# A cached attention step with an MLP gate: the prologue's q product through four PSUM banks, another order of the weight loads and of the gate product, another order at the exit

## The chip, the core and the metric

The kernel runs on one core of one Trainium2 chip. The metric is device time in microseconds (us) of one execution, lower is better. The engines are TensorE (PE in the profile; its weight loads are PEld), VectorE (DVE), ScalarE (ACT), GpSimd (POOL) and SyncE (SP), which here does little but issue DMA transfers. Each engine works through its own instructions in order, and semaphores hold them against each other.

## What is computed

Two sequences of one token each (B = 2, D = 512) go through an attention step over a long cache and, beside it, through a small MLP whose result gates the attention's output:

```
xn = layernorm(x)
q  = xn @ wq                                  # 512 x 4096: 32 heads of 128
p  = softmax(q k^T / sqrt(128));  o = p v     # 8 kv heads, 4 q heads on each, 32768 keys
s  = o @ wo                                   # 4096 x 512
m  = xn + gelu(layernorm(xn) @ w3) @ w4       # the MLP
out = x + s * silu(m)
```

The MLP has a first half with `w1` and `w2`, whose result is shifted along the sequence; with one token that leaves only zeros, so the kernel does not load these weights. k_cache and v_cache are 2 x 8 x 32768 x 128 in bf16, 134 MB each; wq and wo have 4.2 MB each, w3 and w4 1.8 MB each.

## The kernel before, in words

**Groups.** The 16 pairs of a sequence and a kv head are the groups. For each group the kernel loads K (8.4 MB) and V (8.4 MB). K goes into two of the three slots of `kbuf` (a group takes two neighbouring slots, alternately 0 and 1, or 1 and 2); V takes both slots of `vbuf`. In each group, VectorE transposes K in 16 pieces (L632) into four small buffers `T`, TensorE multiplies them with q into two PSUM banks `sc` (L744), VectorE takes maxima (L611) and a row from which the softmax shift follows (L754, L643), ScalarE takes the exponential (L534), VectorE transposes that (L651), TensorE multiplies it with V into the PSUM bank `o` (L766) and sums the weights into the bank `S` (L773), and ScalarE copies `o` out (L539). The head's division and turning (`head_on`, `head_xp`, `head_out`) come one group later.

**The order of the transfers.** SP issues all large transfers on one queue, in the order written down: w3 (L327), w4 (L328), wq (L329), K of group 0 (L330), V of group 0 (L495), four small ones that spread the gate g (L504), and then K and V by turns (L511, L495), at the end wo in six parts (L524, L526). wq lies in slot 2 of `kbuf`, w3 and w4 in `vbuf`. Each issue waits for the buffer that it overwrites:

- V of group 0 waits for the w4 product (`e_h2`, L501), since it overwrites w3 and w4.
- K of group m waits until the first half of group m-1 is through TensorE (L513); K of group 1 waits for `e_q` too, since wq lies under it.
- V of group m waits for ScalarE's signal at L538 that group m-1's product with V is done.

Below, K0, V0, K1, V1 and so on are these transfers, by their group.

**The prologue** (L327 to L506) makes everything that group 0 needs. VectorE clears PSUM banks (L351 to L356), makes two layernorms (L358 to L376) and a number of constant masks. TensorE turns the normalized rows (L416) and makes the w3 product into the bank `pro` (L425). VectorE transposes that out of PSUM (L429) and goes through the gelu (L430 to L437, the tanh on ScalarE at L435). TensorE makes the w4 product into a bank of `sc` (L449 to L451), VectorE and ScalarE make the gate g from it (L452 to L454). Only then the q product: a loop of eight chunks of 512 columns (L463), four matmuls each, through the two `sc` banks by turns; ScalarE copies each chunk into the buffer `q_row` (L477, L479), which GpSimd had cleared (L345); after the last copy VectorE transposes it in four instructions of 32 x 1024 (L481). L483, L487 and L490 bring q into its final form `qr`, from which GpSimd fills the weights `z` of group 0 (L549). `order(m)` says which half of K comes first.

**The exit** (L783 to L817). After the last group TensorE takes the head's last turn (`head_xp`, L785), a product of all earlier heads' outputs named wide (L787), a filler (L790), and then the products with wo (L805, L813), each part as it lands; `own_part` (L672) turns wide into the left operand of the first part on VectorE. wsum (L691) and L795 join the two accumulations; L692, L693 apply the gate and add x; two transfers write the output (L696).

`Queue.op` (L50) adds the waits that an instruction needs and signals a count of its engine; `LateQueue` (L67) keeps TensorE's prologue instructions until `place()` (L730). `take(s, n)` (L411) waits until semaphore s has n and lowers it by n.

Of the kernel before, what the change touches and what calls it, by code (L numbers as in the profile page):

```python
# [21 lines left out]
T_BUFS = 4  # L22
# [109 lines left out]
def kernel(  # L132
# [48 lines left out]
    def sb(name, shape, dt):  # L181
        return pool.tile(shape, dt, name=name)
# [7 lines left out]
    T_all = sb("T", [128, T_BUFS * W], I32)  # L190
    Ts = [T_all[:, i * W:(i + 1) * W] for i in range(T_BUFS)]
# [51 lines left out]
    sc2 = bank("sc", 512 * NPART)  # L243
    sc = [sc2[:, 512 * i:512 * (i + 1)] for i in range(NPART)]
    o = bank("o")
    S = bank("S")
# [56 lines left out]
    qT = kbuf_wq.bitcast(F32)[:, 0:Hq * 32]  # L303
    q_row = T_all[0:32, :].bitcast(F32)
    assert T_BUFS * W == Hq * Dh
# [18 lines left out]
    with tc.tile_critical(sync_engine=mybir.EngineType.Pool, no_gpsimd_drain=True):  # L324
        nc.scalar.wait_ge(t_shift, n_out).then_inc(t_shift, -n_out)

        sp.op(lambda e: e.dma_start(out=vbuf[:, 0:W4O], in_=B_w3.rearrange("(p k) f -> p (k f)", k=DK)), inc=(d_w3, 16))  # L327
        sp.op(lambda e: e.dma_start(out=vbuf[:, W4O:W4O + FK * D], in_=B_w4.rearrange("(p f) d -> p (f d)", f=FK)), inc=(d_w4, 16))  # L328
        sp.op(lambda e: e.dma_start(out=kbuf_wq[:, 0:DK * HD], in_=A_wq.rearrange("(p k) f -> p (k f)", k=DK)), inc=(d_wq, 16))  # L329
# [15 lines left out]
        e_row0 = po.op(lambda e: e.memset(q_row, 0.0))  # L345
# [5 lines left out]
        ve.op(lambda e: e.memset(o[:, :], 0.0))  # L351
        for t in (S[:, 0:NPART * rep], oT[:, :]):
            ve.op(lambda e, t=t: e.memset(t, 1.0), inc=(t_tv, 1))
        e_pro0 = ve.op(lambda e: e.memset(pro[:, :], 0.0))
        ve.op(lambda e: e.memset(sc[0][:, :], 0.0))
        e_s00 = ve.op(lambda e: e.memset(sc[1][:, :], 0.0))  # L356
        nc.vector.sem_inc(t_q, NPART)
# [71 lines left out]
        e = ve.op(lambda v: v.transpose(out=h4[:, :], in_=pro[:, 0:FQ]), e, e_row0)  # L429
# [7 lines left out]
        e = ve.op(lambda v: v.tensor_mul(out=h_bf[:, :], in0=hf[:, :], in1=th[:, :]), e, (d_w4, 16))  # L437
        h2 = sc[1]
# [10 lines left out]
        pe.op(lambda t: t.matmul(h2[0:B, :], lhsT=h_bf[:, 0:B], rhs=w4v[:, 0, :], start=True, stop=False), e, inc=False)  # L449
        pe.loop(nc, (FK - 2) // W4N, w4_part)  # L450
        e_h2 = pe.op(lambda t: t.matmul(h2[0:B, :], lhsT=h_bf[:, (FK - 1) * B:FK * B], rhs=w4v[:, FK - 1, :], start=False, stop=True))  # L451
        e_tf = ve.op(lambda v: v.tensor_add(out=t_f[:, :], in0=xn[:, :], in1=h2[0:B, :]), e_h2)  # L452
        e = ac.op(lambda v: v.activation(out=sig[:, :], in_=t_f[:, :], func=ACT.Sigmoid), e_tf)
        e_g = ve.op(lambda v: v.tensor_mul(out=g[:, :], in0=t_f[:, :], in1=sig[:, :]), e)  # L454

        HC = 512 // Dh
        NC = Hq // HC

        def q_part(t, c):
            take(t, t_q)  # L460
            out_c = sc2[0:B, bass.ds((c & 1) * 512, 512)]
            for k in range(DK):
                ins = t.matmul(  # L463
                    out_c, lhsT=xT[:, k, :], rhs=wq3[:, k, bass.ds(c * 512, 512)],
                    start=(k == 0), stop=(k == DK - 1))
            return ins

        pe.loop(nc, NC, q_part, e_tf, (d_wq, 16), inc=(t_qp, 1))

        def q_out(c):  # L470
            take(nc.scalar, t_qp)
            return q_row[0:B, bass.ds(c * 512, 512)], sc2[0:B, bass.ds((c & 1) * 512, 512)]

        ac.wait(e_row0)
        with nc.Fori(0, NC - 1, engines=[ACTE]) as c:
            dst, src = q_out(c)
            nc.scalar.copy(out=dst, in_=src).then_inc(t_q, 1)  # L477
        dst, src = q_out(NC - 1)
        e = ac.op(lambda v: v.copy(out=dst, in_=src))  # L479
        for n in range(NQ):  # L480
            e = ve.op(lambda v, n=n: v.transpose(  # L481
                out=qT[32 * n:32 * n + 32, :], in_=q_row.rearrange("p (h n y) -> p n h y", n=NQ, y=32)[:, n, :, :]), e, e_row0)
# [372 lines left out]
```

## Time and profile before

| | |
|---|---|
| time, median of 3 runs | 657.93 us (657.11 to 658.06) |
| the profiled execution's own time | 658.21 us |
| its span from the first to the last instruction | 656.4 us |
| busy share of the span: PE, PEld, DVE, ACT, POOL | 65%, 24%, 59%, 7%, 2% |
| DMA: bytes, rate over the span, share of 16 engines on SP's queue | 280.53 MB, 427 GB/s, 98.9% |
| granted TensorE clock, mean | 0.885 |

The span starts with the first instruction; all times of rows are counted from there. A row of the timeline gives the start, the duration, the engine, the line, the operation, the written and the read tile, the shapes, the number of instructions merged into the row, and in brackets how long the engine had been idle and what ended that. A row of the stage table gives the stretch and its length, the busy time of each engine with its number of instructions, and at its end the granted TensorE clock, the DMA engines' share and the rate in GB/s. "DMA share" and GB/s of a short stretch swing because a packet counts where it begins.

### The profile page before, as it was taken

To read this page: it belongs to the slowest core of one execution; us is meant where nothing else is said; L and a number is where in the kernel's file an instruction comes from. 1 tells how busy PE (TensorE), PEld (TensorE's weight loads), DVE (VectorE), ACT (ScalarE), POOL (GpSimd) and SP (SyncE) were. 2 spreads that over 40 slices of the span, in tenths; PEclk is the share of its full clock that TensorE was granted. 3 is DMA by queue.
4 is the path that set the end of the run, shared out by engine and by line. 5 is a ranking of instruction groups with operands and counts; after the bars stand their busy time and mean duration, and the time that the engine had idled before them with its cause. 6 is when DMAs were issued, how large, how long until landed. Compare 5 with 4: busy or idle time off the path is not lost. (4 is left out here: it accounts for less than half of the span.)

```text
span 656.4 us, 6559 instructions
## 1 busy us (share of the span) xinstructions
PE 427.7 (65%) x2411; PEld 160.5 (24%) x2443; DVE 386.9 (59%) x543; ACT 44.3 (7%) x98; POOL 14.0 (2%) x45
## 2 busy tenths in 40 slices
PE   1628687474866757487675748757575875658876
PEld 0103232122322222132222213222222322223323
DVE  6169393573928557292754828376382846738772
ACT  1220101000010000101000010100001010000101
POOL 3000000000000000000000000000000000000000
PEclk9879979698897979889796988969699796969999
DMA  9999999999999999999999999999999999999996
GB/s 374 425 447 448 403 423 443 439 427 423 439 439 443 423 423 443 439 439 427 423 443 435 439 431 419 447 435 435 435 419 443 439 431 435 423 443 415 437 427 263
DMA packets 6246, 280.53 MB, mean 427 GB/s; under 512 B 730, under 2 KB 868, under 8 KB 1380
## 3 DMA queue, kind: packets, MB, share of 16 engines
q1 hardware_dynamic: 6232, 280.50, 98.9%
q8 instruction: 1, 0.02, 0.0%
q14 instruction: 1, 0.01, 0.0%
q10 hardware_dynamic: 12, 0.00, 0.0%
HBM read 280.50 MB, written 0.00 MB: 427 GB/s over the span
## 5 line engine op out<-in xcount | busy, mean ns | idle before, releaser
L632 DVE STREAM_TRANSPOSE T<-kbuf 128x1024 int32<-128x1024 int32 x256 | 296.5, 1214 | 165.0 <-DMA kbuf<-in_A_k_cache_dram 148.4
L744 PE MATMUL sc<-T,z 128*128 128x512 bf16 x992 | 271.9, 421 | 160.9 <-PEq L412 156.6
L744 PEld LDWEIGHTS sc<-T,z 128*128 128x128 bf16 x1024 | 98.5, 103 | 327.6 <-issue 238.5
L766 PE MATMUL o<-vbuf,pt 128*16 128x512 bf16 x1024 | 70.8, 379 | 17.7 <-PEq L412 17.7
L534 ACT ACTIVATE ep<-sc,shift 128x512 bf16<-128x512 f32 x32 | 21.7, 682 | 495.4 <-ACTq L412 495.4
L766 PEld LDWEIGHTS o<-vbuf,pt 128*16 128x16 bf16 x1024 | 27.5, 88 | 64.6 <-issue 42.4
L611 DVE TENSOR_REDUCE mx<-sc 128x1 f32<-128x512 f32 x32 | 21.5, 672 | 34.4 <-PE xp L711 34.4
L718 PE MATMUL pro<-ob,comb 128*2 128x512 f32 x66 | 33.7, 592 | 0.0
L651 DVE STREAM_TRANSPOSE pt<-ep 128x512 bf16<-128x512 bf16 x32 | 22.6, 707 | 15.0 <-ACT ep L534 15.0
L754 PE MATMUL S<-mxr,same_h 128*128 128x448 f32 x32 | 15.8, 576 | 18.3 <-PEq L412 18.3
L705 PEld LDWEIGHTS oT<-sel_o,ob 128*128 128x128 f32 x128 | 15.5, 191 | 11.1 <-issue 11.1
L705 PE MATMUL oT<-sel_o,ob 128*128 128x4 f32 x128 | 16.4, 252 | 0.0
L773 PE MATMUL S<-sm,ones_f 128*128 128x448 f32 x32 | 16.3, 592 | 0.0
L539 ACT COPY ob<-o 128x512 f32<-128x512 f32 x16 | 9.4, 585 | 78.6 <-ACTq L412 78.6
L556 POOL COPY oX<-oXs 128x4 bf16 (+1 forms) x16 | 3.0, 186 | 545.1 <-POOLq L412 545.1
L643 DVE TENSOR_REDUCE shift<-S 128x1 f32<-128x64 f32 x16 | 3.6, 224 | 14.3 <-PE S L754 14.3
L481 DVE STREAM_TRANSPOSE kbuf<-T 32x1024 f32<-32x1024 f32 x4 | 4.9, 1235 | 10.7 <-ACT T L479 10.6
L463 PE MATMUL sc<-kbuf,xT 128*2 x32 | 8.2, 377 | 3.8 <-issue 2.3
L754 PEld LDWEIGHTS S<-mxr,same_h 128*128 128x128 f32 x32 | 4.8, 188 | 22.6 <-issue 22.6
L615 DVE TENSOR_SCALAR mxr<-row_of,mx 128x32 f32<-128x32 f32 x32 | 7.7, 242 | 1.1
L416 PE MATMUL qrb<-ident,xs_bf 34*128 34x34 bf16 x4 | 0.3, 198 | 12.0 <-DVE xs_bf L376 12.0
L718 PEld LDWEIGHTS pro<-ob,comb 128*2 128x2 f32 x66 | 4.2, 83 | 14.0 <-issue 10.4
(106 smaller groups left out, 96.3 us busy)
## 6 DMA issues: line engine op xcount, KB each, us to landing
kbuf<-in_A_k_cache_dram SPq DMA_DIRECT2D x2, 4096.0 KB, 21.9
vbuf<-in_A_v_cache_dram SPq DMA_DIRECT2D x2, 4096.0 KB, 21.2
kbuf<-in_A_wq_dram SPq DMA_DIRECT2D x1, 4096.0 KB, 20.6
vbuf<-in_B_w_dram SPq DMA_DIRECT2D x2, 1792.0 KB, 9.5
kbuf<-in_A_wo_dram SPq DMA_DIRECT2D x1, 2048.0 KB, 30.2
kbuf<-in_A_wo_dram SPq DMA_DIRECT2D x3, 512.0 KB, 31.4
kbuf<-in_A_wo_dram SPq DMA_DIRECT2D x1, 384.0 KB
kbuf<-in_A_k_cache_dram SPq DMA_DIRECT2D x15, 26.7
```

What stands on the lines that cost most here:

```text
L463: ins = t.matmul(out_c, lhsT=xT[:, k, :], rhs=wq3[:, k, bass.ds(c * 512, 512)], start=(k == 0), stop=(k == DK - 1))
L534: nc.scalar.activation(out=ep[i][:, :], in_=sc[i][:, :], func=ACT.Exp, scale=inv_sqrt_dh, bias=shift[:, :], accum_out=rs[:, i:i + 1]).then ...
L539: nc.scalar.copy(out=ob[:, :], in_=o[:, :]).then_inc(t_ob, 1)
L611: ins = nc.vector.tensor_reduce(out=mx[:, i:i + 1], in_=sc[i][:, :], axis=AX.X, op=ALU.max)
L632: ins = nc.vector.transpose(out=Ts[n % T_BUFS][:, :].rearrange("p (b t k) -> p t b k", b=NB, t=RT), in_=kt[:, r * W:(r + 1) * W].rearrange ...
L651: ins = nc.vector.transpose(out=pt[h][:, :, :].rearrange("p r (t h) -> p t r h", h=rep), in_=ep[order(par).index(h)][:, :].rearrange("p (t ...
L705: ins = nc.tensor.matmul(oT[:, :], lhsT=ob[:, t * Dh:(t + 1) * Dh], rhs=sel_o[:, t, :], start=(t == 0), stop=(t == VT - 1))
L718: nc.tensor.matmul(pro[0:B, :], lhsT=comb[:, 0:B], rhs=ob[:, :], start=True, stop=True)
L744: ins = nc.tensor.matmul(sc2[:, bass.ds(i * 512, 512)], lhsT=z[:, nb, w, zc:zc + 128], rhs=Tb[:, nb, :, w], start=(r == 0 and nb == 0 and ...
L754: nc.tensor.matmul(S[:, NPART * rep:NPART * (rep + SREP * 32)].rearrange("p (s c) -> p s c", s=SREP), lhsT=same_h[:, :], rhs=mxr[:, :, :]. ...
L766: ins = nc.tensor.matmul(o[32 * j:32 * j + VT * rep, :], lhsT=pt[h][:, r, a * VT * rep:(a + 1) * VT * rep], rhs=vt[:, u * VT:(u + 1) * VT, ...
L773: nc.tensor.matmul(S[:, 0:SSUM * NPART * rep].rearrange("p (s c) -> p s c", s=SSUM), lhsT=ones_f[:, :], rhs=sm[:, :, :].rearrange("p i h - ...
```

## The change

Four things are changed.

1. **q goes through four PSUM banks, and VectorE takes it from there.** The banks `sc` (2), `o` and `S` become one tile `banks`, and chunk c of the q product goes into bank c mod 4, with room for four at the start. When two chunks are done, VectorE transposes them straight out of PSUM, in four instructions of 32 x 256, into `qT`, which now lies in the first of the `T` buffers; ScalarE's eight copies, `q_row` and GpSimd's clearing of it are gone. The clearing of `S` and `o` moves behind the gate.
2. **The loads are issued in the order w3, wq, w4.**
3. **The gate product (w4) comes behind the q product on TensorE**, into the bank `pro`. On VectorE the gate's operations come behind those of q, up to `qr`.
4. **At the exit the wide product and the filler come ahead of the last head's turn**, and TensorE's extra wait at the end of each group (L779) is gone.

```diff
-    T_all = sb("T", [128, T_BUFS * W], I32)
-    Ts = [T_all[:, i * W:(i + 1) * W] for i in range(T_BUFS)]
+    Ts = [sb(f"T{i}", [128, W], I32) for i in range(T_BUFS)]
...
-    sc2 = bank("sc", 512 * NPART)
+    QB = 4
+    banks = bank("banks", 512 * QB)
+    sc2 = banks[:, 0:512 * NPART]
     sc = [sc2[:, 512 * i:512 * (i + 1)] for i in range(NPART)]
-    o = bank("o")
-    S = bank("S")
+    o, S = (banks[:, 512 * i:512 * (i + 1)] for i in (2, 3))
...
-    qT = kbuf_wq.bitcast(F32)[:, 0:Hq * 32]
-    q_row = T_all[0:32, :].bitcast(F32)
-    assert T_BUFS * W == Hq * Dh
+    qT = Ts[0].bitcast(F32)
...
         sp.op(lambda e: e.dma_start(out=vbuf[:, 0:W4O], in_=B_w3.rearrange("(p k) f -> p (k f)", k=DK)), inc=(d_w3, 16))
+        sp.op(lambda e: e.dma_start(out=kbuf_wq[:, 0:DK * HD], in_=A_wq.rearrange("(p k) f -> p (k f)", k=DK)), inc=(d_wq, 16))
         sp.op(lambda e: e.dma_start(out=vbuf[:, W4O:W4O + FK * D], in_=B_w4.rearrange("(p f) d -> p (f d)", f=FK)), inc=(d_w4, 16))
-        sp.op(lambda e: e.dma_start(out=kbuf_wq[:, 0:DK * HD], in_=A_wq.rearrange("(p k) f -> p (k f)", k=DK)), inc=(d_wq, 16))
...
-        e_row0 = po.op(lambda e: e.memset(q_row, 0.0))
...
-        ve.op(lambda e: e.memset(o[:, :], 0.0))
-        for t in (S[:, 0:NPART * rep], oT[:, :]):
-            ve.op(lambda e, t=t: e.memset(t, 1.0), inc=(t_tv, 1))
         e_pro0 = ve.op(lambda e: e.memset(pro[:, :], 0.0))
-        ve.op(lambda e: e.memset(sc[0][:, :], 0.0))
-        e_s00 = ve.op(lambda e: e.memset(sc[1][:, :], 0.0))
-        nc.vector.sem_inc(t_q, NPART)
+        ve.op(lambda e: e.memset(oT[:, :], 1.0), inc=(t_tv, 1))
+        e_s00 = ve.op(lambda e: e.memset(banks[0:32, :], 0.0), inc=(t_q, QB))
...
-        e = ve.op(lambda v: v.transpose(out=h4[:, :], in_=pro[:, 0:FQ]), e, e_row0)
+        e = ve.op(lambda v: v.transpose(out=h4[:, :], in_=pro[:, 0:FQ]), e)
...
-        e = ve.op(lambda v: v.tensor_mul(out=h_bf[:, :], in0=hf[:, :], in1=th[:, :]), e, (d_w4, 16))
-        h2 = sc[1]
+        e_hb = ve.op(lambda v: v.tensor_mul(out=h_bf[:, :], in0=hf[:, :], in1=th[:, :]), e)
+        HC = 512 // Dh
+        NC = Hq // HC
+        QP2 = 2 * HC
+
+        def q_part(t, c):
+            take(t, t_q)
+            out_c = banks[0:B, bass.ds((c & (QB - 1)) * 512, 512)]
+            for k in range(DK):
+                ins = t.matmul(
+                    out_c, lhsT=xT[:, k, :], rhs=wq3[:, k, bass.ds(c * 512, 512)],
+                    start=(k == 0), stop=(k == DK - 1))
+            return ins
+
+        q_0 = pe.n
+        pe.loop(nc, NC, q_part, e_xT, (d_wq, 16))
+        for c in range(NC // 2):
+            two = banks[0:32, 1024 * (c % 2):1024 * (c % 2) + 1024].rearrange("p (h n y) -> p n h y", n=NQ, y=32)
+            for n in range(NQ):
+                free = c < NC // 2 - QB // 2 and n == NQ - 1
+                e = ve.op(lambda v, c=c, n=n, two=two: v.transpose(
+                    out=qT[32 * n:32 * n + 32, c * QP2 * 32:(c + 1) * QP2 * 32], in_=two[:, n, :, :]),
+                    (pe.sem, q_0 + 2 * c + 2), inc=(t_q, 2) if free else True)
+        e_q = ve.op(lambda v: v.tensor_mul(
+            out=q_sb[:, :, :, :].rearrange("p n e (b h) -> p (n e) b h", b=B),
+            in0=qT[:, :].rearrange("p (h c) -> p c h", c=32)[:, 0:B, :].unsqueeze(1).broadcast_to([128, 2 * NB, B, Hq]),
+            in1=cls[:, :, :].rearrange("p n e -> p (n e)").unsqueeze(2).unsqueeze(3).broadcast_to([128, 2 * NB, B, Hq])), e)
+        h2 = pro
...
-        pe.op(lambda t: t.matmul(h2[0:B, :], lhsT=h_bf[:, 0:B], rhs=w4v[:, 0, :], start=True, stop=False), e, inc=False)
+        pe.op(lambda t: t.matmul(h2[0:B, :], lhsT=h_bf[:, 0:B], rhs=w4v[:, 0, :], start=True, stop=False), e_hb, (d_w4, 16), inc=False)
         pe.loop(nc, (FK - 2) // W4N, w4_part)
         e_h2 = pe.op(lambda t: t.matmul(h2[0:B, :], lhsT=h_bf[:, (FK - 1) * B:FK * B], rhs=w4v[:, FK - 1, :], start=False, stop=True))
-        e_tf = ve.op(lambda v: v.tensor_add(out=t_f[:, :], in0=xn[:, :], in1=h2[0:B, :]), e_h2)
-        e = ac.op(lambda v: v.activation(out=sig[:, :], in_=t_f[:, :], func=ACT.Sigmoid), e_tf)
-        e_g = ve.op(lambda v: v.tensor_mul(out=g[:, :], in0=t_f[:, :], in1=sig[:, :]), e)
-
...
-        pe.loop(nc, NC, q_part, e_tf, (d_wq, 16), inc=(t_qp, 1))
...
-            dst, src = q_out(c)
-            nc.scalar.copy(out=dst, in_=src).then_inc(t_q, 1)
-        dst, src = q_out(NC - 1)
-        e = ac.op(lambda v: v.copy(out=dst, in_=src))
-        for n in range(NQ):
-            e = ve.op(lambda v, n=n: v.transpose(
-                out=qT[32 * n:32 * n + 32, :], in_=q_row.rearrange("p (h n y) -> p n h y", n=NQ, y=32)[:, n, :, :]), e, e_row0)
...
         e = pe.op(lambda t: t.matmul(
             qrb[:, 0:NB * 2 * B * Hq], lhsT=sel[:, :, :].rearrange("p j w -> p (j w)"),
             rhs=q_sb[:, :, :, :].rearrange("p n e c -> p (n e c)"), start=True, stop=True), e_q, e_sel)
         e_qr = ve.op(lambda v: v.tensor_copy(
             out=qr[:, :, :, :, :].rearrange("p n e b h -> p (n e b h)"), in_=qrb[:, 0:NB * 2 * B * Hq]), e)
+        e_tf = ve.op(lambda v: v.tensor_add(out=t_f[:, :], in0=xn[:, :], in1=h2[0:B, :]), e_h2)
+        e = ac.op(lambda v: v.activation(out=sig[:, :], in_=t_f[:, :], func=ACT.Sigmoid), e_tf)
+        e_g = ve.op(lambda v: v.tensor_mul(out=g[:, :], in0=t_f[:, :], in1=sig[:, :]), e)
...
         ve.op(lambda v: v.memset(qrb[:, :], 0.0), e_qr)
+        ve.op(lambda v: v.memset(S[:, 0:NPART * rep], 1.0), inc=(t_tv, 1))
+        e_o0 = ve.op(lambda v: v.memset(o[:, :], 0.0))
         e_s0 = ve.op(lambda v: v.memset(pro[:, :], 0.0))
...
-            ins.then_inc(*((t_vt, 2) if behind else (t_on, 1)))
+            ins.then_inc(t_vt if behind else t_on, 1)
...
-        for s, v in prologue._new((e_s00, e_const, e_hf, e_tf, e_s0)):
+        for s, v in prologue._new((e_o0, e_const, e_hf, e_tf, e_s0)):
...
             head_oT()
-            nc.tensor.wait_ge(t_vt, 2)
             nc.tensor.br_lt(turn, NG, on_true="pe_groups", on_false="pe_output").branch_hint(hint_p)
...
         with nc.body("pe_output", valid_engines=[PE]):
-            take(nc.tensor, t_vt, 2)
-            head_xp()
             pe.wait(e_sp, e_oX[NG - 2])
             pe.op(lambda t: t.matmul(
                 wide, lhsT=sel_w[:, :, :].rearrange("p j w -> p (j w)"), rhs=oX_sp[:, :, :, :, :].rearrange("p k b j r -> p (k b j r)"),
                 start=True, stop=True))
             fill(1)
+            take(nc.tensor, t_vt)
+            head_xp()
```

The loop `q_part` of before and its place are in the kernel above (L456 to L468); its waits for `e_tf` are the reason why the gate came first there.

19 lines of the change are left out of this document (removed).

## The prediction

> **What bounds the kernel now.** I read the page first: its DMA line, its bytes, and the chain that ended last, whose longest piece I take from the chain in order of time (start, duration, what).
>
> ```profile
> span 656.4 us, 6559 instructions
> DMA  9999999999999999999999999999999999999996
> HBM read 280.50 MB, written 0.00 MB: 427 GB/s over the span
> 619.22 33.02 DMA kbuf<-in_A_wo_dram
> ```
>
> The DMA engines are busy from the first slice to the last, and the end hangs on a load of wo that was issued at 619.22 and had to wait in the queue behind K and V until 652.25. So this kernel is a queue of transfers with compute beside it. An edit of compute is worth only what it does to that queue. The second view is the stage table, in stretches of one group's period; the last two columns are the DMA share and GB/s.
>
> ```profile
> 41.75:80.39 38.64, 25.68 (x144) 9.68 (x146) 25.87 (x37) 2.03 (x5) 0.77 (x3) 0.87 1.01 431
> 80.39:119.03 38.64, 26.24 (x143) 9.93 (x145) 22.85 (x30) 2.03 (x5) 0.48 (x2) 0.88 0.99 427
> 119.03:157.66 38.63, 24.93 (x143) 9.50 (x145) 22.68 (x30) 2.03 (x5) 0.48 (x2) 0.90 1.00 434
> 196.30:580.00 383.70, 255.07 (x1430) 96.68 (x1450) 227.43 (x300) 20.31 (x50) 4.79 (x20) 0.87 1.00 434
> ```
>
> 434 GB/s is the steady rate. The first two stretches fall short by 3 and 7 of 434, which over 38.64 us is 0.3 + 0.6 = **0.9 us**. The share of busy engines hides that (0.99). The third view shows the same loss from the other side: the first VectorE instruction of each group, which waits for K to land.
>
> ```profile
> 80.39 2.37 DVE L632 STREAM_TRANSPOSE T<-kbuf 128x1024 int32<-128x1024 int32 x2 [7.35 <-DMA kbuf<-in_A_k_cache_dram]
> 121.03 3.50 DVE L632 STREAM_TRANSPOSE T<-kbuf 128x1024 int32<-128x1024 int32 x3 [12.14 <-DMA kbuf<-in_A_k_cache_dram]
> 159.66 3.50 DVE L632 STREAM_TRANSPOSE T<-kbuf 128x1024 int32<-128x1024 int32 x3 [11.15 <-DMA kbuf<-in_A_k_cache_dram]
> 546.03 2.37 DVE L632 STREAM_TRANSPOSE T<-kbuf 128x1024 int32<-128x1024 int32 x2 [10.13 <-DMA kbuf<-in_A_k_cache_dram]
> ```
>
> K2 to K3 takes 38.63; ten more such periods lead to 546.03 (386.37 / 10 = 38.64). K1 to K2 takes 40.64, **2.0 us more**. Both sizes can be true: a transfer is spread over 16 engines and has landed when the slowest is done, so the mean loss is 0.9 and that of the slowest 2.0. It is never made up, since every later period is 38.64. Why there? The fourth view is SP's own timeline.
>
> ```profile
> 25.45 0.36 SPq L495 DMA_DIRECT2D vbuf<-in_A_v_cache_dram  x1
> 57.06 0.36 SPq L511 DMA_DIRECT2D kbuf<-in_A_k_cache_dram  x1
> 77.09 0.33 SPq L495 DMA_DIRECT2D vbuf<-in_A_v_cache_dram  x1
> 112.93 0.33 SPq L495 DMA_DIRECT2D vbuf<-in_A_v_cache_dram  x1
> 539.95 0.33 SPq L495 DMA_DIRECT2D vbuf<-in_A_v_cache_dram  x1
> ```
>
> I call lead the time from an issue to the landing of the transfer queued ahead of it. V1 (77.09) has 80.39 - 77.09 = 3.3; V2 has 121.03 - 112.93 = 8.1, the V at 539.95 has 6.1, with full rate after both. K1 has 4.0, if V0 lands half a period ahead of K1 (61.07), and no loss can be told there. So a lead of 3.3 is too short, 6.1 is enough, and the point lies between, nearer 4. V1 is late because group 0 is late: nothing but the prologue holds it.
>
> **The change, part by part.** The prologue's rows (the clock is the column ahead of the last two):
>
> ```profile
> 1.14 0.48 DVE L351 MEMSET o<- 128x512 f32 x1 [1.14 <-PEq L839]
> 1.81 0.43 SPq L329 DMA_DIRECT2D kbuf<-in_A_wq_dram  x1
> 3.10 3.50 POOL L345 MEMSET T<- 32x4096 f32 x1
> 4.29 2.59 DVE L358 CAST shared<-x_bf 2x512 f32<-2x512 bf16 x1 [1.01 <-DMA x_bf<-in_A_x_dram]
> 17.77 0.65 DVE L429 STREAM_TRANSPOSE T<-pro 128x448 f32<-128x448 f32 x1 [3.68 <-PE pro L425]
> 20.12 0.38 PE L449 MATMUL sc<-vbuf,h_bf 128*2 128x512 bf16 x1 [2.46 <-DVE h_bf L437]
> 25.04 0.38 PE L451 MATMUL sc<-vbuf,h_bf 128*2 128x512 bf16 x1
> 25.45 0.68 DVE L452 TENSOR_TENSOR shared<-shared,sc 2x512 f32<-2x512 f32 x1 [5.39 <-PE sc L451]
> 26.82 0.68 DVE L454 TENSOR_TENSOR g<-shared 2x512 f32<-2x512 f32 x1 [0.69 <-ACT shared L453]
> 26.86 1.02 PE L463 MATMUL sc<-kbuf,xT 128*2 x4 [1.45 <-PEq L412]
> 28.24 0.57 ACT L477 COPY T<-sc  x1 [1.45 <-ACTq L412]
> 36.36 1.02 PE L463 MATMUL sc<-kbuf,xT 128*2 x4 [0.34 <-issue]
> 38.11 5.04 DVE L481 STREAM_TRANSPOSE kbuf<-T 32x1024 f32<-32x1024 f32 x4 [10.61 <-ACT T L479]
> 43.83 0.40 PE L487 MATMUL qrb<-q_sb,sel 128*128 128x256 bf16 x1 [6.45 <-DVE q_sb L483]
> 45.80 5.80 DVE L632 STREAM_TRANSPOSE T<-kbuf 128x1024 int32<-128x1024 int32 x5
> L443 PE MATMUL sc<-vbuf,h_bf x12: 376/595/634, 20.5 to 24.8; 128*2 x12
> kbuf<-in_A_wq_dram SPq DMA_DIRECT2D x1, 4096.0 KB, 20.6
> 20.00:24.00 4.00, 3.65 (x10) 0.87 (x11) 0.06 (x1) 0.86 (x1) 0.00 (x0) 0.64 1.19 516
> ```
>
> *Start of q.* wq, issued at 1.81, landed 20.6 later, at 22.4, behind w3 and w4. With w4 (1.84 MB, 4.2 us at 434) behind it, it lands at 18.2. TensorE is ready earlier: its w3 product ended before 17.77, and sooner now, since the 2.59 us cast ended just after GpSimd's 3.50 us clearing of `q_row` (6.88 and 6.60), which goes. So q starts at 18.2, not 26.86.
>
> *The q product.* (36.36 - 26.86) / 7 = 1.36 us a chunk, eight take 10.9. A pair of chunks is 2.7 us; its four transposes of 32 x 256 out of PSUM cost 0.46 each by the slope from 1.235 (5.04 / 4, for 1024 columns) to 0.65 (448), and at most that 1.235. At 0.46 a pair's 1.8 hides under TensorE's 2.7; I take that, the nearest row in size and the only one out of PSUM. The gelu stands ahead of them on VectorE and ends before the first pair does (h_bf was there at 20.12, the first pair comes at 20.9). TensorE idles ahead of 18.2, and its clock fell to 0.64 in the stage that followed the idle time ahead of 20.12, where L443's matmuls took 0.595 and not 0.376. Half a chunk time for 3.4 us costs 1.0 more: q ends at 29.1 to 30.1. [...]
>
> *w4 product, V0.* It took 5.3 (20.12 to 25.42), plus 0.5 to enter the loop: it ends at **35 to 36**, and SP issues V0 then, not at 25.45. That is the cost of the move. K0 lands at 80.39 - 38.64 = 41.75, so the lead falls from 16.3 to about 6, which the row at 539.95 shows to be enough.
>
> *q's end.* L487, now behind w4 on TensorE, comes at 36 instead of 43.83. From there to 45.80 were 1.97 us; the gate's VectorE and ScalarE work (25.45 to 27.50, 2.05) and the moved clearings of `S` and `o` (under 0.6 by the 0.48 of L351 at 1.14) now lie on VectorE between. 36 + 2.0 + 2.1 + 0.6 = 40.7, 1 us ahead of K0. So **group 0 starts with K0's landing, 41.75, 4.05 earlier than at 45.80.** The four gate transfers end on SP near 41, K1's issue comes over 10 us later.
>
> *K1 and V1.* V1 moves from 77.09 to 73.0. TensorE comes in colder, so by group 1's own stretch (80.39 to 112.93, 32.5, against 31.3) it is 74.3 at the latest. Lead 6.1 to 7.4 instead of 3.3: full rate. K1's lead goes from 4.0 to 7 or more.
>
> *At nothing:* the order w3, wq, w4 moves the same bytes; ScalarE's copies, GpSimd's clearing and the extra wait at the end of a group (its value is waited for at the next loop's head anyway) stand beside DMA-bound time. Without that cover each would cost its own row, 0.57 a copy. *The exit:*
>
> ```profile
> 651.35 0.39 PE L805 MATMUL qrb<-kbuf,oX 128*2 128x512 bf16 x4 [0.81 <-DMA kbuf<-in_A_wo_dram]
> 652.38 0.50 PE L813 MATMUL pro<-kbuf,oXz 128*4 128x128 bf16 x12 [0.65 <-DMA kbuf<-in_A_wo_dram]
> ```
>
> Starting the products with wo some 0.4 us sooner lengthens these two waits for wo and moves nothing. If wo came earlier than the products, it would be worth up to that 0.4.
>
> **The sum.** What comes back at V1 is 0.9 us if the mean engine counts and 2.0 if the slowest does. The kernel ends on a landing, so I take 1.8, near the upper end, since not all of the two landings' difference need last to the end. 658.21 (span 656.4 and 1.8 outside it) - 1.8 = 656.4; the profiled execution lay 0.28 above the median, so **656.1** against 657.93, 0.27%. A measurement of this kernel can tell about 0.2%, 1.3 us, from no change.
>
> **The rivals.** *Nothing comes back.* The loss near 80 may not hang on V1's lead: K1's lead of 4.0 showed none, and one short lead is one case. Then the time stays at 657.9; with the mean loss alone it is 657.0. [...] Against this rival stands that the rate is full wherever the lead is 6.1 or more. Chance 0.27. *V0 comes late (slower).* The price of V0 behind q: it is paid from a w4 product that ends after 41.75 - 3.3 = 38.4. TensorE's last two chunks need the banks of the second pair, so the product ends at 20.9 + two pairs of transposes + 2.7 + 5.8, and 38.4 is reached at 4.5 a pair, 1.1 a transpose. At 1.235 it ends at 39.2: V0's lead is 2.5, 0.8 less than the one that costs 2.0. VectorE ends the fourth pair at 40.6, and group 0 starts at 45 or later as before, so V1's loss stays too: 657.9 + 2.8 = 660.7. Against it: 1.235 is for four times the columns. Chance 0.06. *The exit counts as well:* 655.7, inside the forecast. *The change doesn't do what it says:* q comes early, but group 0 does not, because VectorE's queue behind q is longer than 40.7; then V1's lead stays under 4 and it is the first rival again.
>
> **How the numbers follow.** The forecast with or without the exit has 0.67, nothing back or the mean alone 0.27, V0 late 0.06. The range reaches from 655.3 (2.0 and the exit's 0.4, with some scatter) to 658.1 (nothing back); V0's case is left out. Faster by over 0.2%, under 656.6: 0.67. Within: 0.27. Slower: 0.06.
>
> **What would show it.** V1 issued at 73 to 74.3 and V0 at 35 to 36; group 0's first transposes at 41.75; K1 to K2 in 38.6 instead of 40.6; 434 GB/s from 42 on; the last wo landing near 650.4. Wrong it is if K1 to K2 stays near 40.6 though V1 was early, or if group 0 starts at 43 or later, or if a new slow period shows at V0.

## The result, and the profile after

The changed kernel took 656.64 us (median of 16 runs, 656.03 to 658.61), the kernel before beside it 658.02 (16 runs, 657.02 to 658.80): a ratio of **0.9983, with a 95% interval of 0.9975 to 0.9992**. That is 1.1 us faster by the ratio, 1.4 by the medians. The profiled execution was one of its long ones, 658.30 with a span of 656.5; this matters for the exit, below. First the page, then the landing of K (the first VectorE rows of groups 0 to 3), then SP's issues, all of the kernel after.

```profile
span 656.5 us, 6538 instructions
DMA  8999999999999999999999999999999999999995
HBM read 280.50 MB, written 0.00 MB: 427 GB/s over the span
```

```profile
41.73 5.84 DVE L621 STREAM_TRANSPOSE T<-kbuf 128x1024 int32<-128x1024 int32 x5 [2.91 <-DMA kbuf<-in_A_k_cache_dram]
80.33 5.83 DVE L621 STREAM_TRANSPOSE T<-kbuf 128x1024 int32<-128x1024 int32 x5 [10.72 <-DMA kbuf<-in_A_k_cache_dram]
119.00 5.83 DVE L621 STREAM_TRANSPOSE T<-kbuf 128x1024 int32<-128x1024 int32 x5 [11.14 <-DMA kbuf<-in_A_k_cache_dram]
157.61 5.83 DVE L621 STREAM_TRANSPOSE T<-kbuf 128x1024 int32<-128x1024 int32 x5 [11.38 <-DMA kbuf<-in_A_k_cache_dram]
```

```profile
34.53 0.36 SPq L482 DMA_DIRECT2D vbuf<-in_A_v_cache_dram  x1
53.72 0.35 SPq L500 DMA_DIRECT2D kbuf<-in_A_k_cache_dram  x1
73.66 0.33 SPq L482 DMA_DIRECT2D vbuf<-in_A_v_cache_dram  x1
```

Group 0 now waits 2.91 us for K0 and starts with its landing, at 41.73. V1 is issued at 73.66, a lead of 80.33 - 73.66 = 6.7 us. The landings of K are 38.60, 38.67 and 38.61 apart: the step of 40.64 is gone. The stage table (its last column is GB/s) no longer has the two short stretches of 431 and 427:

```profile
41.75:80.39 38.64, 26.24 (x145) 9.88 (x145) 22.81 (x31) 2.03 (x5) 0.48 (x2) 0.85 1.00 434
80.39:119.03 38.64, 25.75 (x145) 9.72 (x145) 22.73 (x31) 2.03 (x5) 0.48 (x2) 0.85 1.00 434
```

K3 lands 159.66 - 157.61 = 2.05 us earlier than before. Yet the span is no shorter: 656.5 against 656.4. What was won at 119 is lost again at the exit. Its TensorE rows, then two rows of the stage table (the granted clock is the third number from the end):

```profile
649.32 0.39 PE L793 MATMUL qrb<-kbuf,oX 128*2 128x512 bf16 x4 [0.85 <-DMA kbuf<-in_A_wo_dram]
651.84 0.81 PE L801 MATMUL pro<-kbuf,oXz 128*4 128x128 bf16 x12 [2.14 <-DMA kbuf<-in_A_wo_dram]
652.44 1.06 PE L783 MATMUL pro<-T,comb 128*4 128x128 f32 x8
653.29 0.42 PE L801 MATMUL pro<-kbuf,oXz 128*4 128x128 bf16 x4
```

```profile
650.00:652.00 2.00, 0.16 (x4) 0.19 (x6) 0.00 (x0) 0.34 (x1) 0.00 (x0) 0.66 0.06 14
652.00:654.00 2.00, 1.71 (x24) 1.11 (x20) 0.25 (x1) 0.00 (x0) 0.00 (x0) 0.50 0.00 0
```

The last part of wo lands at 651.71, only 0.5 us earlier than the 652.25 of before. TensorE waits 2.14 us for it (0.65 before), and then runs its last 24 matmuls at half clock (0.50 in the second stretch; the kernel before has 1.00 in the same one): the twelve of L801 take 0.81 and not 0.50.

So two things need a cause: the steps of K's landings, and the exit.

### The profile page after: what moved, and what is told of

It reads as the page before. It is cut to its first block, busy times and chain, and to the rows that moved or that the text cites. A ratio compares the mean times of both kernels' runs of the same rounds, so it can differ in the third digit from the quotient of the medians.

```text
span 656.5 us, 6538 instructions
## 1 busy us (share of the span) xinstructions
PE 433.2 (66%) x2443; PEld 161.9 (25%) x2443; DVE 387.6 (59%) x554; ACT 39.7 (6%) x90; POOL 10.3 (2%) x44
## 5 line engine op out<-in xcount | busy, mean ns | idle before, releaser
L733 PE MATMUL banks<-T,z 128*128 128x512 bf16 x1024 | 276.7, 424 | 163.2 <-PEq L405 161.1
L733 PEld LDWEIGHTS banks<-T,z 128*128 128x128 bf16 x1024 | 99.6, 104 | 333.5 <-issue 245.8
L755 PE MATMUL banks<-vbuf,pt 128*16 128x512 bf16 x1024 | 70.4, 379 | 17.7 <-PEq L405 17.7
L523 ACT ACTIVATE ep<-banks,shift 128x512 bf16<-128x512 f32 x32 | 21.7, 682 | 494.6 <-ACTq L405 494.6
L755 PEld LDWEIGHTS banks<-vbuf,pt 128*16 128x16 bf16 x1024 | 27.3, 88 | 64.9 <-issue 42.7
L600 DVE TENSOR_REDUCE mx<-banks 128x1 f32<-128x512 f32 x32 | 21.5, 672 | 34.4 <-PE xp L700 34.4
L743 PE MATMUL banks<-mxr,same_h 128*128 128x448 f32 x32 | 15.8, 577 | 18.3 <-PEq L405 18.3
L762 PE MATMUL banks<-sm,ones_f 128*128 128x448 f32 x32 | 16.3, 593 | 0.0
L528 ACT COPY ob<-banks 128x512 f32<-128x512 f32 x16 | 9.4, 585 | 78.6 <-ACTq L405 78.6
L439 PE MATMUL banks<-kbuf,xT 128*2 x32 | 9.4, 440 | 4.7 <-PEq L405 3.3
L743 PEld LDWEIGHTS banks<-mxr,same_h 128*128 128x128 f32 x32 | 4.8, 188 | 22.6 <-issue 22.6
```

The lines of the kernel that those rows point to most:

```text
L439: ins = t.matmul(out_c, lhsT=xT[:, k, :], rhs=wq3[:, k, bass.ds(c * 512, 512)], start=(k == 0), stop=(k == DK - 1))
L523: nc.scalar.activation(out=ep[i][:, :], in_=sc[i][:, :], func=ACT.Exp, scale=inv_sqrt_dh, bias=shift[:, :], accum_out=rs[:, i:i + 1]).then ...
L528: nc.scalar.copy(out=ob[:, :], in_=o[:, :]).then_inc(t_ob, 1)
L600: ins = nc.vector.tensor_reduce(out=mx[:, i:i + 1], in_=sc[i][:, :], axis=AX.X, op=ALU.max)
L733: ins = nc.tensor.matmul(sc2[:, bass.ds(i * 512, 512)], lhsT=z[:, nb, w, zc:zc + 128], rhs=Tb[:, nb, :, w], start=(r == 0 and nb == 0 and ...
L743: nc.tensor.matmul(S[:, NPART * rep:NPART * (rep + SREP * 32)].rearrange("p (s c) -> p s c", s=SREP), lhsT=same_h[:, :], rhs=mxr[:, :, :]. ...
```

## The experiments

The kernel before ran beside each, and each ratio is taken against these runs. Its medians were 658.31 (26 runs) beside the repeat, the four banks, the exit alone and n = 13; 658.29 (22) beside all but the exit, the wait put back, the wait taken away and n = 9; 658.40 (15) beside the order alone, n = 7 and V0 held back; 657.53 (one run) beside the third profile. Theory A (the prediction's): a transfer issued too shortly before its predecessor lands costs the slowest of the engines time that never comes back. Its rival: the loss at 80 has another cause in the prologue. Theory B, formed on the profile after: the new exit costs what the profile shows there. Its rival: the long profiled execution is chance, and the exit costs nothing.

### The same kernel again, and a third profile

No edit; the file of the changed kernel.

> The changed kernel once more. Theory (V1's lead): K1 to K2 takes 38.6 us again, and the time is 0.2% to 0.3% below before, about 656.4. Second question, the end: in the first profile of this kernel the last part of wo landed at 651.7, 1.4 us after the other engines were done, on an engine that also carried one packet of 16 KB of instructions at 649.4. If that meeting is a matter of chance, this profile shows either the same or, without it, a last landing near 650.4 and a span near 654.4; if it belongs to the kernel, the span is 656.5 again.

656.70 us (10 runs, 655.82 to 658.25), ratio 0.9976 (0.9966 to 0.9987). Seven runs lie between 655.8 and 656.9, three at 657.87 or more, the profiled one (658.07) among these.

> The changed kernel a third time, for its profile alone. Of its 26 timed executions 8 took 657.3 or more, and both profiles so far are of such executions. Theory on the end: a shorter execution shows the last wo landing near 650.4, the last wait for wo near 0.7 us and TensorE at full clock, with a span near 654.3; a longer one shows the packet of instructions ahead of wo's last data again, the wait of 2 us or more and the half clock behind it, with a span of 656.3 or more.

One run, 658.02. In both profiles the exit looks as in the first: waits of 2.33 and 2.17 us for the last part of wo, and 0.81 for the twelve. So all three profiled executions of this kernel are of the long kind, though only 8 of its 26 timed runs took 657.3 us or more. No short execution of it was profiled, so what its exit looks like there isn't known.

### One part alone: the four banks

On the changed kernel, parts 2, 3 and 4 are undone (the w4 product and the gate go ahead of the q product again, still in the bank `pro`):

```diff
-        sp.op(lambda e: e.dma_start(out=kbuf_wq[:, 0:DK * HD], in_=A_wq.rearrange("(p k) f -> p (k f)", k=DK)), inc=(d_wq, 16))
         sp.op(lambda e: e.dma_start(out=vbuf[:, W4O:W4O + FK * D], in_=B_w4.rearrange("(p f) d -> p (f d)", f=FK)), inc=(d_w4, 16))
+        sp.op(lambda e: e.dma_start(out=kbuf_wq[:, 0:DK * HD], in_=A_wq.rearrange("(p k) f -> p (k f)", k=DK)), inc=(d_wq, 16))
...
+        h2 = pro
...
+        pe.loop(nc, (FK - 2) // W4N, w4_part)
...
+        e_g = ve.op(lambda v: v.tensor_mul(out=g[:, :], in0=t_f[:, :], in1=sig[:, :]), e)
...
         pe.loop(nc, NC, q_part, e_xT, (d_wq, 16))
...
-        h2 = pro
...
-        pe.loop(nc, (FK - 2) // W4N, w4_part)
...
-        e_g = ve.op(lambda v: v.tensor_mul(out=g[:, :], in0=t_f[:, :], in1=sig[:, :]), e)
...
-            ins.then_inc(t_vt if behind else t_on, 1)
+            ins.then_inc(*((t_vt, 2) if behind else (t_on, 1)))
+            nc.tensor.wait_ge(t_vt, 2)
             nc.tensor.br_lt(turn, NG, on_true="pe_groups", on_false="pe_output").branch_hint(hint_p)
+            take(nc.tensor, t_vt, 2)
+            head_xp()
...
-            take(nc.tensor, t_vt)
-            head_xp()
```

> Part 1 alone: q through four banks with VectorE taking it from there, but w3, w4, wq in the old order, the gate product ahead of q's, and the old exit. Theory: q starts near 24 once wq has landed at 22.4, ends near 35, group 0's first transposes come with K0's landing at 41.75, V1 is issued near 73.5 and K1 to K2 takes 38.6, so the whole gain comes from this part: about 656.4. Rival (the order of the loads or of the products is needed): group 0 starts at 43 or later and K1 to K2 stays over 39.5, about 657.5.

655.79 us (5 runs, 655.70 to 656.47), ratio 0.9965 (0.9951 to 0.9978). Its landings of K1 and K2 and its exit:

```profile
80.49 4.62 DVE L622 STREAM_TRANSPOSE T<-kbuf 128x1024 int32<-128x1024 int32 x4 [11.41 <-DMA kbuf<-in_A_k_cache_dram]
119.17 4.62 DVE L622 STREAM_TRANSPOSE T<-kbuf 128x1024 int32<-128x1024 int32 x4 [10.29 <-DMA kbuf<-in_A_k_cache_dram]
650.48 0.50 PE L803 MATMUL pro<-kbuf,oXz 128*4 128x128 bf16 x12 [0.62 <-DMA kbuf<-in_A_wo_dram]
```

The four banks alone start group 0 at 41.88 and bring 2.3 us by the ratio. The exit is that of before: a wait of 0.62, the twelve in 0.50.

### One part alone: the order of loads and products

The kernel before with parts 2 and 3 alone: wq is loaded second, the q product (two banks, ScalarE's copies, `q_row`) comes ahead of the w4 product, which goes into `pro`, and the gate's operations follow `qr`.

```diff
+        sp.op(lambda e: e.dma_start(out=kbuf_wq[:, 0:DK * HD], in_=A_wq.rearrange("(p k) f -> p (k f)", k=DK)), inc=(d_wq, 16))
         sp.op(lambda e: e.dma_start(out=vbuf[:, W4O:W4O + FK * D], in_=B_w4.rearrange("(p f) d -> p (f d)", f=FK)), inc=(d_w4, 16))
-        sp.op(lambda e: e.dma_start(out=kbuf_wq[:, 0:DK * HD], in_=A_wq.rearrange("(p k) f -> p (k f)", k=DK)), inc=(d_wq, 16))
...
-        h2 = sc[1]
+        h2 = pro
...
-        pe.loop(nc, (FK - 2) // W4N, w4_part)
...
-        pe.loop(nc, NC, q_part, e_tf, (d_wq, 16), inc=(t_qp, 1))
+        pe.loop(nc, NC, q_part, e_xT, (d_wq, 16), inc=(t_qp, 1))
...
+        pe.loop(nc, (FK - 2) // W4N, w4_part)
```

> The kernel before with parts 2 and 3 alone: loads in the order w3, wq, w4 and the gate product behind q's, in the bank of w3's; q still goes through two banks and ScalarE's copies into q_row, with GpSimd's clearing of it. Theory: q starts at 18.5 to 19, its last copy ends near 31, the four long transposes near 36, TensorE's w4 product near 35.5, so group 0 again starts with K0's landing at 41.75, V1 is issued at 73 to 74.5, K1 to K2 takes 38.6 and the time is 655.8 to 656.1: either half of the change is enough. If VectorE's long transposes push the start past 43.5, K1 to K2 is over 39 and the time 657.

656.09 us (5 runs, 655.88 to 656.17), ratio 0.9963 (0.9949 to 0.9976); K lands at 41.46, 80.06, 118.73. **Either half starts group 0 with K0's landing and brings the whole gain; the two together bring no more.**

### One part alone: the exit

The kernel before with part 4:

```diff
-            ins.then_inc(*((t_vt, 2) if behind else (t_on, 1)))
+            ins.then_inc(t_vt if behind else t_on, 1)
...
-            nc.tensor.wait_ge(t_vt, 2)
...
-            take(nc.tensor, t_vt, 2)
-            head_xp()
...
             fill(1)
+            take(nc.tensor, t_vt)
+            head_xp()
```

> The old kernel with part 4 alone, the exit's order. Theory: nothing before the last group changes, K1 to K2 stays at 40.6, the waits for wo at the end get 0.4 us longer and the time is that of before, 657.9 to 658.0. Rival (the gain comes from the exit): 656.6 with K1 to K2 at 40.6.

658.96 us (11 runs, 658.39 to 661.32), ratio 1.0014 (1.0005 to 1.0023): **slower by 0.9 us.** Its exit, and SP's and VectorE's rows near 80:

```profile
653.27 0.81 PE L812 MATMUL pro<-kbuf,oXz 128*4 128x128 bf16 x12 [1.84 <-DMA kbuf<-in_A_wo_dram]
```

```profile
57.83 0.36 SPq L511 DMA_DIRECT2D kbuf<-in_A_k_cache_dram  x1
77.64 0.33 SPq L495 DMA_DIRECT2D vbuf<-in_A_v_cache_dram  x1
```

```profile
81.92 5.83 DVE L632 STREAM_TRANSPOSE T<-kbuf 128x1024 int32<-128x1024 int32 x5 [8.32 <-DMA kbuf<-in_A_k_cache_dram]
120.73 5.83 DVE L632 STREAM_TRANSPOSE T<-kbuf 128x1024 int32<-128x1024 int32 x5 [11.54 <-DMA kbuf<-in_A_k_cache_dram]
```

The exit shows the long wait and the half clock here too, without the rest of the change. Besides, the loss near 80 has moved: K1 was late this time (issued 57.83, a lead of some 3.2 before V0's landing, taken half a period, 19.3, after K0's 41.7) and landed near 40.2 after K0; V1 had a lead of 81.92 - 77.64 = 4.28, and the step after it is 38.81. So the 0.9 sets a smaller loss near 80 against the price of the exit: K3 landed 0.30 earlier than before (159.36 against 159.66).

### All but the exit

The changed kernel with part 4 undone (the last hunks of the first diff above):

> Parts 1 to 3 of the change with the exit and the group's end as they were before. Theory (V1's lead gives the whole gain, parts 2 and 3 neither add nor take): group 0 starts at 41.75, K1 to K2 takes 38.6, and the time is that of part 1 alone, 655.8. Theory on the end: with the old exit the packet of instructions comes at 650 or later, after the wo data of its engine, the last wait for wo stays near 0.6 us, and all executions lie within 655.6 to 656.6. Rival (parts 2 and 3 cost something, for instance through V0's shorter lead): 656.4 or more.

656.06 us (6 runs, 655.70 to 656.22), ratio 0.9969 (0.9958 to 0.9981). The last part of wo lands at 650.29 (617.30 + 32.99 in the chain). Against the medians of the changed kernel's two series the new exit thus costs 0.6 us, beside the 0.9 of the exit alone; theory B stands and its rival falls. The size is known loosely: the ratio's interval here overlaps those of the changed kernel's two series.

### One wait put back, and one wait taken away

The new order at the exit, but TensorE may leave the group loop only when `t_vt` has come:

```diff
+            nc.tensor.wait_ge(t_vt, 1)
             nc.tensor.br_lt(turn, NG, on_true="pe_groups", on_false="pe_output").branch_hint(hint_p)
```

> The changed kernel with its new exit, and one wait put back: at the end of each group TensorE waits for one count of VectorE's semaphore ahead of its branch, which in the last group holds it until VectorE has written the head's division, some 1 us. Theory on the end (TensorE's branch out of the group loop asks for 16 KB of instructions, which then come in among the last packets of wo): the packet comes later than 649.4, its meeting with wo's last parts goes or gets rare, and the median falls from 656.7 to 655.8 to 656.2. Rival (the new order of the products itself costs): 656.7 with executions over 657.5 among them, as in the changed kernel.

656.06 us (7 runs, 655.69 to 656.80), ratio 0.9973 (0.9962 to 0.9984), and in the profile:

```profile
650.40 0.50 PE L802 MATMUL pro<-kbuf,oXz 128*4 128x128 bf16 x12 [0.62 <-DMA kbuf<-in_A_wo_dram]
```

```profile
650.00:652.00 2.00, 1.05 (x24) 0.82 (x24) 0.47 (x2) 0.42 (x1) 0.00 (x0) 1.00 0.05 16
```

The order of the products is that of the changed kernel, and the long wait and the half clock are gone. The other way round, the four banks alone (above) without the wait at L779:

```diff
-            nc.tensor.wait_ge(t_vt, 2)
             nc.tensor.br_lt(turn, NG, on_true="pe_groups", on_false="pe_output").branch_hint(hint_p)
```

> Part 1 alone with the old order at the exit, but without the wait at the group's end, so that TensorE branches out of the loop earlier. Theory on the end: the packet of instructions comes 0.5 to 1 us earlier against the last data of wo, and some executions are 1.4 to 2 us longer, as in the changed kernel: median 656.2 to 656.8, spread over 1.5 us. Rival (the order of the products costs, not the branch): 655.8 within 0.8 us, as part 1 alone.

656.05 us (8 runs, 655.74 to 657.16), ratio 0.9972 (0.9961 to 0.9983). Two of the eight runs lie at 657.1 and 657.2, the profile shows the short exit, and the median is below the 656.2 to 656.8 that was expected. So the missing wait alone wasn't shown to be enough: whether the long exit comes now and then with the old order of the products stays open.

What delays wo? The list of DMA queues in short windows and the single packets behind it show it. In the kernel after, 649.3 to 650.3, and then 650.32 to 651.7 (packets, MB, share of the 16 engines):

```profile
q1 hardware_dynamic: 52, 0.06, 17.7%
q8 instruction: 1, 0.02, 5.8%
```

```profile
q1 hardware_dynamic: 13, 0.02, 4.8%
```

One packet of instructions, 16,384 bytes by its record, runs from 649.38 to 650.31, 0.93 us (5.8% of 16 engines over 1.00 us), among the last packets of wo. By 650.24 every other packet of wo is done; one that starts at 650.30 and the 13 of the second row are left, one after the other, until 651.62, and TensorE waits for these. The records don't name the engine of a packet; but the one at 650.30 starts as the packet of instructions ends, and the rest follow it end to start, so they are taken for the work of the engine that carried it. With the wait put back, the window 650.1 to 651.5 reads:

```profile
q8 instruction: 1, 0.02, 4.2%
q1 hardware_dynamic: 12, 0.01, 2.0%
```

Here the packet starts at 650.24, when its engine has no wo left, and delays nothing. In the kernel before it falls into the window 650.4 to 650.7 (first row), while wo still lands until 652.25 (second row, 651.6 to 652.3):

```profile
q8 instruction: 1, 0.02, 19.4%
```

```profile
q1 hardware_dynamic: 12, 0.01, 5.6%
```

It ran from 650.66 to 651.59, and no packet of wo starts at its end, so its engine is taken to have been done; the twelve packets behind 651.6 follow each other without a gap, as the work of one other engine (it may be the one that lost 2 us at 80; that isn't shown). The landings agree. From K3's landing to that of the last wo took 492.59 before, 492.58 in the four banks alone, 492.58 without the exit and with the wait put back, but 494.10 in the changed kernel and 493.77 in the exit alone.

All 14 profiles of this case have one such packet near the end. In four of them (the three of the changed kernel and the exit alone) a packet of wo starts at its end, and wo is late; in the other ten none does. The new order without the wait is in these four and in one of the ten, n = 13 below, where the packet came at 652.48, TensorE waited 0.63 for the last part and the twelve took 0.50. So with that exit the meeting came in four of five profiles.

That the packet is TensorE's own, fetched because it leaves its loop, was only argued. The wait put back fits it in part: the packet came at 650.24 and not at 649.38, but 0.58 of these 0.86 are the last group itself, whose copy of `o` on ScalarE starts at 643.66 and not at 643.08. The wait taken away doesn't fit it: there the packet came at 650.30, no earlier than the 650.17 of the four banks with the wait. No record names the engine that fetched it, and what sets its start stays open.

### The lead, in doses

The changed kernel, and then the one without the exit, with group 0 held back by clearings of `pro` on VectorE, one after the other, ahead of the first transposes; n is 13, 9 and 7:

```diff
+        e = None
+        for _ in range(n):
+            e = ve.op(lambda v: v.memset(pro[:, :], 0.0), e)
-        e_s0 = ve.op(lambda v: v.memset(pro[:, :], 0.0))
+        e_s0 = ve.op(lambda v: v.memset(pro[:, :], 0.0), e)
```

> The changed kernel, with thirteen more clearings of a PSUM bank on VectorE ahead of group 0, 0.54 us each by the row, so that group 0 starts near 45.85, as in the kernel before; everything else of the change stays. Theory: V1 is issued near 77.7, lead 2.6 us, K1 to K2 takes 40.6 or more and the time is back at 658 or a little over. Rival (the loss near 80 us has nothing to do with V1's lead): K1 to K2 stays at 38.6 and the time at 656.6.

n = 13: 659.45 us (11 runs, 658.18 to 660.74), ratio 1.0025 (1.0016 to 1.0035). The dose was larger than planned: each clearing took 0.67 (0.48, and 0.18 of waiting for the one before), so group 0 started at 48.09 and not at 45.85. K1 was late by it too. The step from K3 to K4 took 39.08 in this run, though the leads there were over 7 us; the lead doesn't explain these 0.4.

```profile
59.73 0.36 SPq L503 DMA_DIRECT2D kbuf<-in_A_k_cache_dram  x1
79.81 0.33 SPq L482 DMA_DIRECT2D vbuf<-in_A_v_cache_dram  x1
```

```profile
81.68 5.83 DVE L624 STREAM_TRANSPOSE T<-kbuf 128x1024 int32<-128x1024 int32 x5 [5.92 <-DMA kbuf<-in_A_k_cache_dram]
121.74 5.83 DVE L624 STREAM_TRANSPOSE T<-kbuf 128x1024 int32<-128x1024 int32 x5 [12.20 <-DMA kbuf<-in_A_k_cache_dram]
```

> Parts 1 to 3 with the old exit, and nine more clearings on VectorE ahead of group 0, which put its start to about 43.7, 2 us after K0's landing. Theory: K1 is issued near 55.5 (lead 5.6 to V0's landing near 61.1), V1 near 75.6 (lead 4.7), and since the run of the old kernel with lead 4.0 at K1 lost nothing, K1 to K2 takes 38.6 to 38.8 and the time is that of the kernel without these clearings, 655.8 to 656.0. If the point from which it costs lies over 4.7, K1 to K2 takes 39 to 40.

n = 9, without the exit: 656.33 us (12 runs, 655.86 to 658.38), ratio 0.9975 (0.9966 to 0.9984). The profiled execution took 657.46:

```profile
76.97 0.33 SPq L482 DMA_DIRECT2D vbuf<-in_A_v_cache_dram  x1
```

```profile
80.41 4.62 DVE L624 STREAM_TRANSPOSE T<-kbuf 128x1024 int32<-128x1024 int32 x4 [7.49 <-DMA kbuf<-in_A_k_cache_dram]
120.38 4.62 DVE L624 STREAM_TRANSPOSE T<-kbuf 128x1024 int32<-128x1024 int32 x4 [12.12 <-DMA kbuf<-in_A_k_cache_dram]
```

A lead of 3.44 and a step of 39.97. The profiled execution was longer than most: the median is only 0.3 above the same kernel without clearings, and the runs spread over 2.5. Either the loss varies from one execution to the next near the point, or the lead does; only this one was profiled.

> As the run with nine clearings, with seven: at the 0.67 us that each took there (0.48 and a wait of 0.18), group 0 starts near 43.75, K1 is issued near 55.6 (lead 5.5) and V1 near 75.6 (lead 4.8). In the runs so far leads of 3.3 to 3.4 cost and leads of 4.0 to 4.3 cost nothing or 0.2 us. Theory: K1 to K2 is 38.6 to 38.7 and the time 655.8 to 656.1. If the point from which it costs lay higher for V than for K, K1 to K2 is 39 or more.

n = 7, without the exit: 655.67 us (5 runs, 655.62 to 656.01), ratio 0.9959 (0.9945 to 0.9972).

```profile
74.49 0.33 SPq L482 DMA_DIRECT2D vbuf<-in_A_v_cache_dram  x1
```

```profile
79.97 4.62 DVE L624 STREAM_TRANSPOSE T<-kbuf 128x1024 int32<-128x1024 int32 x4 [9.53 <-DMA kbuf<-in_A_k_cache_dram]
118.65 4.62 DVE L624 STREAM_TRANSPOSE T<-kbuf 128x1024 int32<-128x1024 int32 x4 [10.83 <-DMA kbuf<-in_A_k_cache_dram]
```

A lead of 5.5, a step of 38.68: no loss, though group 0 started at 43.31, nearly 2 us after K0's landing (taken as 79.97 - 38.6). So the time hangs on the lead and not on the start of group 0.

### Another transfer late

The kernel without the exit, with two more clearings (n = 2 above) and V0's issue held until the last one of the row is done:

```diff
-        load_v(0, e_h2)
...
+        load_v(0, e_h2, e_s0)
```

> Parts 1 to 3 with the old exit, and V0's issue held back until VectorE's last clearing ahead of group 0, with two more clearings of 0.67 us each ahead of that: V0 at about 40.5 instead of 34.5, 1.2 us ahead of K0's landing at 41.75; group 0 itself still starts at 41.75. This prices the slower rival of the prediction. Theory (a lead under 3.3 costs at whichever transfer it falls): K0 to K1 takes 40.0 to 40.8 instead of 38.6, K1 to K2 38.6, and the time is 657.2 to 658. If only V1's place were special, K0 to K1 stays at 38.6 and the time at 656.

657.54 us (11 runs, 657.08 to 658.09), ratio 0.9987 (0.9978 to 0.9996), 1.5 above the kernel that it was made from.

```profile
40.06 0.36 SPq L482 DMA_DIRECT2D vbuf<-in_A_v_cache_dram  x1
73.27 0.33 SPq L482 DMA_DIRECT2D vbuf<-in_A_v_cache_dram  x1
```

```profile
41.36 5.83 DVE L624 STREAM_TRANSPOSE T<-kbuf 128x1024 int32<-128x1024 int32 x5 [1.33 <-DMA kbuf<-in_A_k_cache_dram]
81.42 4.62 DVE L624 STREAM_TRANSPOSE T<-kbuf 128x1024 int32<-128x1024 int32 x4 [12.19 <-DMA kbuf<-in_A_k_cache_dram]
120.17 4.62 DVE L624 STREAM_TRANSPOSE T<-kbuf 128x1024 int32<-128x1024 int32 x4 [10.31 <-DMA kbuf<-in_A_k_cache_dram]
```

Now the long step is that from K0 to K1, 40.06, and V1's is 38.75. The cases together, each from one profiled execution and with the step of K's landings in which the late transfer lies (38.65 is the usual step):

| transfer, kernel | lead, us | step of K's landings, us | longer than 38.65 by, us |
|---|---|---|---|
| V0, held back | 1.3 | 40.06 | +1.4 |
| K1, n = 13 | 1.3 | near 40.0 | near +1.3 |
| V1, n = 13 | 1.87 | 40.06 | +1.4 |
| K1, exit alone | near 3.2 | near 40.2 | near +1.5 |
| V1, before | 3.3 | 40.64 | +2.0 |
| V1, n = 9 | 3.44 | 39.97 | +1.3 |
| V1, exit alone | 4.28 | 38.81 | +0.2 |
| V1, n = 7 | 5.5 | 38.68 | 0 |
| V1, after | 6.7 | 38.67 | 0 |

The rows with "near" take K0's landing as 41.7, V0's as 19.3 later; in these two kernels group 0 starts after K0 has landed, and the landing isn't seen. The loss comes at whichever transfer is late, so theory A stands and its rival falls. It is not in proportion: under some 4 us it is 1.3 to 2.0, whether the lead is 1.3 or 3.4. Why it stops at 4 and why it is that large stays open.

## Why the prediction came out as it did

Rows of the kernel after that answer to the prologue's steps (TensorE and VectorE, from 18 to 39 us):

```profile
18.80 5.31 PE L439 MATMUL banks<-kbuf,xT 128*2 x16 [3.33 <-PEq L405]
22.09 1.86 DVE L450 STREAM_TRANSPOSE T<-banks 32x256 f32<-32x256 f32 x4 [4.36 <-PE banks L439]
28.55 1.02 PE L439 MATMUL banks<-kbuf,xT 128*2 x4 [0.34 <-issue]
34.43 0.28 PE L471 MATMUL qrb<-q_sb,sel 128*128 128x256 bf16 x1
38.34 0.48 DVE L495 MEMSET pro<- 128x512 f32 x1
```

- **The prologue: right, with slack.** q ran from 18.80 to 29.57 (18.2, and 29.1 to 30.1 were forecast), a transpose took 1.86 / 4 = 0.46 as forecast. The 3.4 us at half clock are what the kernel before shows (a granted clock of 0.50 from 21.13 to 24.54, and of 1.00 in the 3.4 us on either side), and they came here too (0.50 from 19.2 to 22.6). The 1.0 for them was too high: the granted clock was 0.65 from 18 to 22, yet the first four chunks took 5.67 (the fifth starts at 24.47), 0.2 over four at 1.36; the later ones came 1.36 apart (24.47, 25.83, 27.19, 28.55). The row of `qrb` came at 34.43 and not at 36: q ended 0.5 ahead of the 30.1, and the w4 product took 5.1 (29.41 to 34.50) with no half microsecond to enter its loop; VectorE was free at 38.82 and not at 40.7. V0 was issued at 34.53 (35 to 36). All of that slack ends at K0's landing, so group 0 starts at 41.73 (41.75).
- **V1's lead: right.** V1 at 73.66 (73.0 to 74.3), steps of 38.67, 434 GB/s. The doses and V0 held back show that the lead is the cause, and place the point between 3.44 and 4.28 us, as the prediction had it.
- **The gain of 1.8: mis-sized, a little low.** It was put between the mean engine's 0.9 and the slowest one's 2.0. The slowest counts in full: 40.64 - 38.67 = 1.97 at the landing, 2.0 and 2.3 us by the ratios without the exit and with the four banks alone, and V0 held back lengthened its step by 1.4 and the time by 1.5.
- **The exit at nothing: this step failed.** "Starting the products with wo some 0.4 us sooner lengthens these two waits for wo and moves nothing" took wo's landing as given. It moved: 651.71 and not 650.4, where the kernel without the exit has 650.29. The prediction priced the new exit by what TensorE does next, and not by what else then runs on the DMA engines. The price is 0.6 to 0.9 us, of both parts: wo late by 1.5 (494.10 against 492.58) and the last products at half clock, some 0.8 (from wo's landing to the issue of the output 2.67 and not 1.85). These 2.3 are what the profiled, long execution shows; most executions are shorter, and the medians show less.
- **The sum.** 656.1 came from 1.8 and nothing; measured are 2.0 to 2.3 gained and 0.6 to 0.9 lost, 1.1 to 1.4 in all and 656.64. The two errors run against each other, so that the time came out within 0.6 of the forecast is partly luck. Whether the gain is over the 0.2% to which the prediction gave 0.67 isn't settled: it is 0.17% by the ratio, whose interval holds both sides, and 0.21% by the medians. Without the exit the time is 656.06: there the forecast stands.
- **The rivals.** "Nothing comes back" falls: the runs show 1.3 to 2.0 us lost at each lead from 1.3 to 3.44, and nothing at 5.5 and 6.7. "V0 late" didn't come about, and its price was too high: 2.8 was named for a lead of 2.5, and V0 at 1.3 cost 1.4.

The version to keep is one with early leads and without the new exit, or with its wait put back: 655.79 (the four banks alone), 656.06, 656.06 and 656.09, below both kernels. The four banks and the new order are each enough, and the new order of the products at the exit, with the wait, brings nothing over the old one (656.06 both).

## What to carry to other kernels

In a kernel bound by its transfers, list for each queued transfer the time from its issue to the landing of the one ahead, and the steps between landings: here the step that was longer than the rest showed what the end lost (2.0 us), and the mean rate showed half of it (0.9). Past the needed lead (between 3.44 and 4.28 us here) an earlier issue was worth nothing (steps of 38.68 at 5.5 and 38.67 at 6.7), so the two halves that each gave it didn't add up (655.79 and 656.09 alone, 656.06 together without the exit). An edit at the end of the program is to be judged by the landing of the last transfer too: here, with a new order and a wait taken away, a packet of instructions came in among the last packets of wo in four of five profiles, and in the changed kernel wo landed 1.5 us later for it.

## What was not expected of the hardware

- One packet of instructions of 16,384 bytes took 0.93 us (the kernel after, 649.38 to 650.31); the packets of wo that followed at its end came slower at first (three of 3,072 bytes took 0.34, 0.34 and 0.21 us; the next one 0.12). In the kernel before, no packet of wo started at the end of such a packet (650.66 to 651.59), and it cost nothing.
- A transfer issued 1.3 to 3.44 us ahead of its predecessor's landing lost 1.3 to 2.0 us, one issued 4.28 us ahead 0.2. At 3.44 the times spread over 2.5 us (655.86 to 658.38).
- Clearings of one tile on VectorE, each made to wait for the one before, came 0.67 apart and not 0.48 (n = 13, from 39.02 on): each ran 0.48, and 0.18 went by idle ahead of it.
